# Two kept buffers for the preparation of w_out, earlier stores of its plain forms, and new block names in an attention and feed-forward kernel

## The chip, the cores and the metric

The kernel runs on one core of a Trainium2 chip. The metric is device time in microseconds of one execution, as the median of several runs. The core has a matmul engine (TensorE, PE; its weight loads are listed as PEld), a vector engine (VectorE, DVE), a scalar engine (ScalarE, ACT), a general engine (GpSimd, POOL) and a queue engine (SyncE, SP) that here only issues DMAs.

## What is computed

```
scores = (q @ k^T) / sqrt(64) - log(448)          # 8 batches, 12 heads, 448 positions, 64 wide
attn   = sigmoid(scores) @ v                      # 3584 tokens x 768
h      = attn @ w_in                              # 768 -> 2048
g      = max(0.01 * h, h)
out    = g @ w_out                                # 2048 -> 768
```

All inputs and the output are float32. The weights come to the kernel as 64-bit words and are turned into float32 on the chip.

## The kernel before, in words

**Number format.** Every operand of a large matmul is split into a high part (a cast on ScalarE) and a low part (the difference, on VectorE), and each product is three matmuls: high by high, high by low, low by high (`parts_mm`). A matmul has 448 columns.

**Fewer products.** Both weight matrices are multiplied by schemes that need fewer block products than the plain one, at the price of sums of blocks. For w_in (stage 2) a quad of four results takes seven products (`ORDER`, class `Quad`). For w_out (stage 3) 24 forms, blocks of w_out and sums of them, meet operands that are blocks of `g` and sums of them, in 26 products for each half of the tokens; the tables `PRODUCTS`, `MADE`, `STEPS` and `BLOCKS` say which. `MADE[p % 2]` lists the sums of `g` blocks (`s0` to `s7`) that stage 2 makes and stores for stage 3.

**Three stages in the order of program, cut in slots.**
1. Attention: 24 rounds of five slots, two head pairs each (tiles `qk`, `qks`, `sc`, `s`, `pv`, `x`).
2. First weight (class `First`): four groups `q` of 56 slots; a slot is nine matmuls, two slots a product, seven products a quad `u` of four. It loads prepared w_in forms (`wx`), splits them (`w`), and its results (`c11`, `c21`, `c22`, `c12`, shown as `c_h`) go through the leaky maximum on ScalarE and are stored to the DRAM tensors `g`. Sums of them (`MADE`, tiles `s`) are made on VectorE some slots later, by `later`, and stored too. Both kinds of tile share `st`, a pool of seven buffers. In the last quad of each group the sums are put off by `LATER` = 4 slots (`z`). The stores of the very last quad go on ScalarE's DMA queue, all others on SP's.
3. Second weight: 52 products of 36 matmuls, alternating between the PSUM accumulators `A` and `B`. The forms of w_out are loaded from the DRAM tensor `t1` (shown as `t`), the operands from `g`; `load`, `whole` (the sum, tile `gf`), `high` and `low` make an operand ready. The first operands are loaded and split in the last slots of stage 2 (list `todo`); the buffers they use are seven (`gp`), and eight more (`op`) that take the place of stage 2's tiles.

**The preparation of the weights** (`prep`) runs on VectorE beside stages 1 and 2, a few instructions a slot. For each of 8 parts `u` of w_in, then of w_out, it loads four raw pieces (`wr`), decodes each with five instructions into a quarter of the tile `wd`, forms sums and stores them: `firsts` for w_in, `second` for w_out. `second` walks through `STEPS`; `("sum", n, fn, to, x, y)` makes `n` blocks of 192 columns, side `d` is the decoded tile `wd` and side `s` the tile `ws`; `("store", side, i, n, form)` stores `n` blocks as forms from `form` on; `("wait",)` is a pause. In the kernel before, `wd` and `ws` are taken anew from a pool of two buffers for each `u`, all decoding comes first, then the first sums, then two stores of eight blocks, the pause, sums written over the blocks of `wd`, and a third store of eight blocks.

**What sets the order.** Each engine runs its instructions in the order of program (`keep_in_program_order`), and so does SP with its DMAs; semaphores make an instruction wait for data and for buffers. The generator `prep` yields after every instruction, and empty turns are yielded in a pause: `rest()` gives `WAIT` = 9 of them before slot 100 and `REST` = 4 after. `prepare` (attention) and `fill` (stage 2) ask the generator for its next turns: `fill` up to four times in a slot, as long as its running account of VectorE's work, `queue`, is under 1.6 us.

Of the kernel before, what the change touches and what calls it, by code (L numbers as in the profile page):

```python
# [10 lines left out]
F32 = mybir.dt.float32  # L11
# [17 lines left out]
READY, LEAD = 2, 2  # L29
# [1 line left out]
PACES = 4, 5, 4.2, 2.8, 2  # L31
TIMES = 1.92, 1.92, 2.33, 2.33, 1.66
PRODUCT, LESS, MOST = 1.8, 0.2, 4
WAIT, REST = 9, 4
ALONE = 100
LATER = 4
IDLE = 7
# [4 lines left out]

RAW = "00", "01", "30", "31", "10", "11", "20", "21"
MADE = (
    (("s0", "add", "30", "31"), ("s1", "add", "10", "20"), ("s2", "add", "00", "30"), ("s3", "add", "s0", "00"), ("s4", "add", "s3", "01")),
    (("s0", "add", "10", "20"), ("s1", "add", "20", "21"), ("s2", "add", "30", "31"), ("s3", "add", "00", "30"), ("s4", "add", "s0", "21"), ("s5", "add", "s2", "00"), ("s6", "add", "s5", "01"), ("s7", "add", "s4", "11")))


PRODUCTS = (
# [13 lines left out]
FORMS = 24  # L63
BLOCKS = "01", "20", "31", "10", "21", "00", "11", "30"
STEPS = (
# [12 lines left out]


def part(i):  # L80
# [14 lines left out]
def attn_ffn_kernel(ctx: ExitStack, tc: tile.TileContext, qk, v, w_in, w_out, out):  # L95
# [66 lines left out]
    def later(slots, *fns, first=False):  # L162

        chores.setdefault(now + slots, ([], []))[not first].extend(fns)
# [182 lines left out]
    def rest():  # L347

        return (None for _ in range(WAIT if now < ALONE else REST))

    def second(u, dec):


        n = len(BLOCKS)
        size = wide // 2
        e, at = u // 2, u % 2 * size
        both = {"d": dec.rearrange("p a b -> p (a b)").rearrange("p (n m) -> p n m", n=n),
                "s": block(F32, (n, size), f"ws1_{u}")}

        def of(n, side, at, step):  # L360
            x = both[side]
            if step == 0:
                return x[:, at:at + 1].broadcast_to((P, n, size))
            end = at + (n - 1) * step + (1 if step > 0 else -1)
            return x[:, at:end if end >= 0 else None:step]

        for what, *x in STEPS:
            if what == "wait":
                yield from rest()
            elif what == "store":  # L370
                side, i, n, form = x
                dma(out=t2d[:, form:form + n, e, at:at + size], in_=both[side][:, i:i + n])
            else:
                n, fn, *x = x
                to, x, y = (of(n, *z) for z in x)
                if fn == "neg":
                    vec_st(out=to, in0=x, scalar=-1.0, in1=y, op0=ALU.mult, op1=ALU.subtract)
                else:
                    (add if fn == "add" else sub)(to, x, y)
                yield  # L380

    def prep():
# [21 lines left out]
        yield  # L404
        for at, (m, k) in enumerate(pieces):
            w, u = todo[m]
            if k == 0:
                dec = block(F32, (4, HW), f"wd{w}_{u}")
            raw = raws[at]
            size = 4 * HW // n  # L410
            low, high = raw[:, :, 0], raw[:, :, 1]
# [13 lines left out]
                load()  # L425
            if now < ALONE:
                yield
            if k < n - 1:
                continue
            if w == 1:  # L430
                yield from second(u, dec)
            else:
                yield from firsts(u, dec)
            prepared.add((w, u))
            yield from rest()

    preps = prep()
    credit = 0.0
# [240 lines left out]
    class First:  # L679
# [26 lines left out]
        def after(self, quad, c, u, n):  # L706
# [21 lines left out]
            if n != 2:  # L728
                later(1, lambda: leaky(t, t))
            later(2 if n == 2 else 3, lambda: save(name(row, col), t))  # L730
            z = LATER if u == NU // 2 - 1 else 0
            have = set(c)
            i = 0
            for x in MADE[p % 2]:
# [135 lines left out]
    class Operand:  # L870
# [28 lines left out]
                else:  # L899
                    y.count[x] += 1  # L900

        def load(self):
            for x in self.new:
                h = self.raw[x] = Held(f"g{x}_{self.k}")
                dma(out=h.t.bitcast(F32), in_=gd[2 * self.p + int(x[0])][x[1:]])

# [70 lines left out]
    def g_load(k):  # L977

        nonlocal ahead
        room = SPARE + sum(x.needs() for x in operands[:k + 5] if x.x is None)  # L980
        while ahead < min(k + FAR + 1, total) and len(spare) >= len(operands[ahead].new) + room:
            operands[ahead].load()
            ahead += 1

# [1 line left out]
    todo = [(operands[k], "load") for k in range(READY)]  # L986
    for k in range(READY):
        todo += [(operands[k], what) for what in ("whole", "high", "low")]
    todo += [(operands[READY], "load")]
    ahead = READY + 1  # L990

    for k in range(NOP, size):
        m, at = divmod(k - NOP, 12)
        if m < WW[0] and at == 0:
            for n, what in ((0, "load"), (5, "high"), (7, "low")):
                later(n, getattr(weights[m], what))
        if k >= size - LEAD - len(todo) and todo:
            later(0, lambda x=todo.pop(0): getattr(*x)())
        slot(first.step)
    assert not todo  # L1000
    while chores:
# [142 lines left out]
```

## Time and profile before

| | |
|---|---|
| median of 3 runs | 1075.38 us (1072.38 to 1076.88) |
| profiled execution, its own time | 1073.51 us |
| its span | 1071.7 us |
| granted TensorE clock, mean | 0.986 |
| busy: PE, PEld, DVE, ACT | 1039.7, 870.3, 842.2, 583.7 us |
| HBM | 202.77 MB read, 96.86 MB written, 280 GB/s over the span |

In the profile's rows `out<-in` are the program's tile names without their numbers, and L132 is the line of the helper that records nearly every instruction, so rows are told apart by tiles. `t<-wd` and `t<-ws` are the stores of prepared weight forms, `g<-c_h` and `g<-s` those of stage 2's results and of their sums. In a timeline's row the bracket gives the idle time of the engine before the instruction and what ended it. A DMA group gives the size of each and the median time from issue to landing.

### The profile page before, as it was taken

Reading aid. Unit: us, or ns where it says so; the run is one execution under the profiler, and the core shown is the slowest. Engines: PE = TensorE matmul, PEld = TensorE weight load, DVE = VectorE, ACT = ScalarE, POOL = GpSimd, SP = SyncE. Lnnn points to the kernel's source line nnn. Section 1 sums busy time; section 2 is a strip of 40 time slices with the busy share of each in tenths; the row PEclk is TensorE's granted clock in tenths of the full one; section 3 lists DMA queues with packets and bytes.
Section 4 is the critical chain, followed back from the end, with each engine's and each line's share of the span. In section 5 each row is a group of like instructions: output and inputs, shape, how many; then the busy total and the mean of one; then the engine's idle time right before and its main releaser. Section 6 shows DMA issues by size and latency. Waiting matters only on the chain.

```text
span 1071.7 us, 15049 instructions
## 1 busy us (share of the span) xinstructions
PE 1039.7 (97%) x5738; PEld 870.3 (81%) x5738; DVE 842.2 (79%) x976; ACT 583.7 (54%) x610; POOL 0.3 (0%) x5
## 2 busy tenths in 40 slices
PE   9999999978999999998999999979999999999998
PEld 5555555534998999987989999969999999999997
DVE  5778888656979998977965566578998888899883
ACT  6877778756544754544545555555444625544440
POOL 0000000000000000000000000000000000000000
PEclk9999999988999999998999999989999999999999
DMA  8888788678789989989886788996669798666923
GB/s 302 286 286 280 258 269 291 233 263 266 264 269 320 324 290 305 341 307 345 278 288 209 255 298 295 363 392 273 255 227 310 276 368 332 267 255 229 312 110 128
DMA packets 113335, 300.62 MB, mean 280 GB/s; under 512 B 9200, under 2 KB 51312, under 8 KB 113264
## 3 DMA queue, kind: packets, MB, share of 16 engines
q1 hardware_dynamic: 111248, 295.19, 77.9%
q10 hardware_dynamic: 2016, 4.47, 1.1%
q8 instruction: 45, 0.74, 0.3%
q14 instruction: 26, 0.21, 0.1%
HBM read 202.77 MB, written 96.86 MB: 280 GB/s over the span
## 4 chain that ended last, share of the span: by engine, by line
PE 85%; DVE 6%; DMA 6%; issue 1%; ACT 1%; SPq 0%; ACTq 0%; DVEq 0%
PE px_h L132 19%; PE acc_B L132 17%; PE acc_A L132 16%; PE pv L132 10%; PE sc L132 9%; PE pz_h L132 8%; PE py_h L132 5%; DMA t<-wd 3%; DMA g<-s 2%; DVE wd L132 2%; DMA wx<-t 1%; DVE w L132 1%; DVE s L132 1%; DVE c_h L132 1%; DVE gf L132 1%
## 5 line engine op out<-in xcount | busy, mean ns | idle before, releaser
L132 PE MATMUL px_h<-hi,w 128*128 128x448 f32 x768 | 229.0, 369 | 12.3 <-DVE c_h L132 6.6
L132 PEld LDWEIGHTS px_h<-hi,w 128*128 128x128 f32 x768 | 146.9, 192 | 25.8 <-issue 8.5
L132 PE MATMUL acc_A<-gh,w 128*128 128x448 f32 x528 | 151.7, 362 | 0.0
L132 PE MATMUL px_h<-lo,w 128*128 128x448 f32 x384 | 141.0, 367 | 0.0
L132 DVE TENSOR_TENSOR w<-wx,w 128x768 fp32r<-128x768 f32 x112 | 106.8, 954 | 42.6 <-ACT w L132 42.5
L132 ACT ACTIVATE s<-sc 128x896 f32<-128x896 f32 x144 | 119.7, 932 | 18.3 <-PE sc L132 18.3
L132 PE MATMUL acc_B<-gh,w 128*128 128x448 f32 x416 | 121.8, 367 | 5.6 <-ACT o L132 4.9
L132 PE MATMUL pv<-s,v 128*64 128x448 f32 x576 | 113.8, 543 | 0.0
L132 PE MATMUL pz_h<-hi,w 128*128 128x448 f32 x384 | 113.2, 362 | 0.0
L132 PEld LDWEIGHTS sc<-qks 64*128 64x128 f32 x876 | 81.6, 190 | 32.0 <-issue 16.9
L132 PE MATMUL sc<-qks 64*128 64x448 f32 (+1 forms) x876 | 97.7, 373 | 7.9 <-DVE qks L132 7.6
L132 PEld LDWEIGHTS acc_A<-gh,w 128*128 128x128 f32 x528 | 98.9, 187 | 6.5 <-ACT o L132 0.4
L132 ACT ACTIVATE c_h<-c_h 128x896 f32<-128x896 f32 x48 | 45.8, 954 | 97.3 <-DVE c_h L132 97.3
L132 ACT CAST w<-wx 128x768 fp32r<-128x768 f32 x112 | 91.7, 833 | 8.0 <-DMA wx<-t 8.0
L132 DVE TENSOR_TENSOR w<-w 128x1536 fp32r<-128x1536 f32 x52 | 91.0, 1752 | 0.0
L132 PEld LDWEIGHTS pv<-s,v 128*64 128x64 f32 x576 | 39.1, 137 | 63.3 <-issue 54.3
L132 PEld LDWEIGHTS acc_B<-gh,w 128*128 128x128 f32 x416 | 79.3, 191 | 11.5 <-ACT o L132 5.3
L132 PE MATMUL acc_B<-g,w 128*128 128x448 f32 x328 | 85.8, 365 | 0.0
L132 PEld LDWEIGHTS px_h<-lo,w 128*128 128x128 f32 x384 | 73.6, 192 | 4.7
L132 ACT CAST w<-w 128x1536 fp32r<-128x1536 f32 x52 | 76.6, 1475 | 0.1
L132 PEld LDWEIGHTS pz_h<-hi,w 128*128 128x128 f32 x384 | 71.9, 188 | 5.1
L132 DVE SCALAR_TENSOR_TENSOR wd<-wr,wd 128x384 int32<-128x384 int32 x128 | 71.3, 557 | 3.3
(98 smaller groups left out, 1583.3 us busy)
## 6 DMA issues: line engine op xcount, KB each, us to landing
wx<-t SPq DMA_DIRECT2D x112, 384.0 KB, 5.1
w<-t SPq DMA_DIRECT2D x52, 768.0 KB, 4.3
g<-g SPq DMA_DIRECT2D x34, 896.0 KB, 7.3
g<-c_h SPq DMA_DIRECT2D x60, 448.0 KB, 4.7
g<-s SPq DMA_DIRECT2D x48, 448.0 KB, 5.3
qk<-in_qk SPq DMA_DIRECT2D x46, 448.0 KB, 5.2
g1s<-g SPq DMA_DIRECT2D x18, 896.0 KB, 6.6
wr<-in_w_in SPq DMA_DIRECT2D x32, 384.0 KB, 4.9
```

What stands on the lines that cost most here:

```text
L132: return lambda *args, **kw: tc.keep_in_program_order(issue(*args, **kw))
```

## The change

`second` gets two buffers that are taken once, for `u` = 0, and swapped for each following `u`: what was side `s` is decoded into next. It is called after each decoded piece `k`: `PLAIN` says that nothing follows piece 0, that blocks 0 to 3 are stored as they are after piece 1, and blocks 4 and 5 after piece 2; `STEPS` follows piece 3. `STEPS` has 14 sums where it had 12, over the same 18 blocks, and five stores; with those of `PLAIN` a part `u` has seven stores of 192 to 576 KB where it had three of 768 KB, and the same 24 blocks. `REST` is 1, and no rest follows a part of w_out. The blocks of w_out have another order (`BLOCKS`), the blocks of results other names in `PRODUCTS`, and the sums of odd groups in `MADE` are made from other blocks; the number and shapes of products and sums in stages 2 and 3 are the same. The last quad of the last group no longer puts its sums off. `todo` loads two more operands (the second only in its first block), so all of `todo` begins two slots earlier.

```
-WAIT, REST = 9, 4
+WAIT, REST = 9, 1
...
 MADE = (
-    (("s0", "add", "30", "31"), ("s1", "add", "10", "20"), ...),
-    (("s0", "add", "10", "20"), ("s1", "add", "20", "21"), ("s2", "add", "30", "31"), ("s3", "add", "00", "30"), ("s4", "add", "s0", "21"), ("s5", "add", "s2", "00"), ("s6", "add", "s5", "01"), ("s7", "add", "s4", "11")))
+    (("s0", "add", "30", "31"), ("s1", "add", "20", "10"), ...),
+    (("s0", "add", "21", "11"), ("s1", "add", "11", "10"), ("s2", "add", "31", "30"), ("s3", "add", "01", "31"), ("s4", "add", "s0", "10"), ("s5", "add", "s2", "01"), ("s6", "add", "s5", "00"), ("s7", "add", "s4", "20")))
...
-    (4, "A", True, ("+1s4",), ("c010", "c100", "c110")), (16, "B", True, ("+001",), ("c101",)),
+    (9, "A", True, ("+1s4",), ("c011", "c100", "c111")), (17, "B", True, ("+001",), ("c101",)),
...
-BLOCKS = "01", "20", "31", "10", "21", "00", "11", "30"
+BLOCKS = "00", "01", "21", "30", "10", "11", "20", "31"
+PLAIN = {0: (), 1: (("store", "d", 0, 4, 0),), 2: (("store", "d", 4, 2, 4),)}
 STEPS = (
-    ("sum", 3, "sub", ("s", 0, 1), ("d", 0, 1), ("d", 2, 1)),
-    ("sum", 1, "neg", ("s", 3, 1), ("d", 3, 1), ("d", 6, 1)),
-    ("sum", 2, "sub", ("s", 4, 1), ("d", 6, 0), ("s", 1, -1)),
-    ("sum", 1, "sub", ("s", 6, 1), ("s", 4, 1), ("d", 4, 1)),
-    ("sum", 1, "sub", ("s", 7, 1), ("s", 0, 1), ("s", 1, 1)),
-    ("sum", 1, "sub", ("d", 3, 1), ("d", 3, 1), ("d", 5, 1)),
-    ("sum", 1, "neg", ("d", 2, 1), ("d", 7, 1), ("d", 2, 1)), ("store", "s", 0, 8, 0), ("store", "d", 0, 8, 8),
-    ("wait",), ("sum", 1, "add", ("d", 4, 1), ("d", 2, 1), ("d", 4, 1)),
-    ("sum", 2, "neg", ("d", 7, -6), ("d", 3, -2), ("d", 7, -3)),
-    ("sum", 2, "add", ("d", 2, 1), ("d", 2, 1), ("d", 0, 6)),
-    ("sum", 1, "neg", ("d", 5, 1), ("d", 2, 1), ("d", 5, 1)),
-    ("sum", 2, "sub", ("d", 6, -6), ("d", 4, -4), ("d", 7, -4)), ("store", "d", 0, 8, 16))
+    ("sum", 3, "sub", ("s", 5, 1), ("d", 1, 3), ("d", 7, -1)), ("store", "s", 5, 3, 11),
+    ("sum", 2, "sub", ("s", 3, 1), ("d", 2, 0), ("s", 6, -1)),
+    ("sum", 1, "sub", ("s", 1, 1), ("s", 5, 1), ("s", 6, 1)),
+    ("sum", 1, "sub", ("s", 2, 1), ("s", 3, 1), ("d", 5, 1)),
+    ("sum", 1, "neg", ("s", 0, 1), ("d", 6, 1), ("d", 2, 1)), ("store", "s", 0, 5, 6),
+    ("sum", 1, "sub", ("d", 6, 1), ("d", 6, 1), ("d", 0, 1)),
+    ("sum", 1, "neg", ("d", 7, 1), ("d", 3, 1), ("d", 7, 1)), ("store", "d", 6, 2, 14), ("wait",),
+    ("sum", 1, "add", ("d", 5, 1), ("d", 7, 1), ("d", 5, 1)),
+    ("sum", 2, "neg", ("d", 3, 1), ("d", 6, -2), ("d", 3, 2)),
+    ("sum", 1, "add", ("d", 2, 1), ("d", 6, 1), ("d", 2, 1)),
+    ("sum", 1, "add", ("s", 7, 1), ("d", 7, 1), ("d", 1, 1)),
+    ("sum", 1, "sub", ("d", 1, 1), ("d", 1, 1), ("d", 2, 1)),
+    ("sum", 1, "neg", ("d", 0, 1), ("s", 7, 1), ("d", 0, 1)),
+    ("sum", 1, "sub", ("s", 6, 1), ("d", 5, 1), ("d", 3, 1)), ("store", "d", 0, 6, 16), ("store", "s", 6, 2, 22))
...
-    def second(u, dec):
+    def second(u, k, dec):
...
-        both = {"d": dec.rearrange("p a b -> p (a b)").rearrange("p (n m) -> p n m", n=n),
-                "s": block(F32, (n, size), f"ws1_{u}")}
+        both = {side: dec[i].rearrange("p a b -> p (a b)").rearrange("p (n m) -> p n m", n=n) for i, side in enumerate("ds")}
...
-        for what, *x in STEPS:
+        for what, *x in PLAIN.get(k, STEPS):
...
-            if k == 0:
+            if k == 0 and w == 0:
                 dec = block(F32, (4, HW), f"wd{w}_{u}")
+            elif k == 0:
+                both = [block(F32, (4, HW), f"wd{w}_{i}") for i in range(2)] if u == 0 else both[::-1]
+                dec = both[0]
...
-            if k < n - 1:
-                continue
             if w == 1:
-                yield from second(u, dec)
-            else:
+                yield from second(u, k, both)
+            elif k == n - 1:
                 yield from firsts(u, dec)
-            prepared.add((w, u))
-            yield from rest()
+            if k == n - 1:
+                prepared.add((w, u))
+                if w == 0:
+                    yield from rest()
...
-            z = LATER if u == NU // 2 - 1 else 0
+            z = LATER if u == NU // 2 - 1 and p < NQ - 1 else 0
...
-        def load(self):
-            for x in self.new:
+        def load(self, n=None):
+            for x in self.new[len(self.raw):n]:
...
-        while ahead < min(k + FAR + 1, total) and len(spare) >= len(operands[ahead].new) + room:
+        while ahead < min(k + FAR + 1, total) and len(spare) >= len(operands[ahead].new) - len(operands[ahead].raw) + room:
...
-    todo += [(operands[READY], "load")]
-    ahead = READY + 1
+    todo += [(operands[READY + n], "load", *part) for n, part in ((0, ()), (1, ()), (2, (1,)))]
+    ahead = READY + 2
...
-            later(0, lambda x=todo.pop(0): getattr(*x)())
+            later(0, lambda x=todo.pop(0): getattr(*x[:2])(*x[2:]))
```

More of the change, by code (lines that the diff above doesn't have):

```diff
@@ L44 @@
 MADE = (
-    (("s0", "add", "30", "31"), ("s1", "add", "10", "20"), ("s2", "add", "00", "30"), ("s3", "add", "s0", "00"), ("s4", "add", "s3", "01")),
-    (("s0", "add", "10", "20"), ("s1", "add", "20", "21"), ("s2", "add", "30", "31"), ("s3", "add", "00", "30"), ("s4", "add", "s0", "21"), ("s5", "add", "s2", "00"), ("s6", "add", "s5", "01"), ("s7", "add", "s4", "11")))
+    (("s0", "add", "30", "31"), ("s1", "add", "20", "10"), ("s2", "add", "00", "30"), ("s3", "add", "s0", "00"), ("s4", "add", "s3", "01")),
+    (("s0", "add", "21", "11"), ("s1", "add", "11", "10"), ("s2", "add", "31", "30"), ("s3", "add", "01", "31"), ("s4", "add", "s0", "10"), ("s5", "add", "s2", "01"), ("s6", "add", "s5", "00"), ("s7", "add", "s4", "20")))
 PRODUCTS = (
[13 rows of a table removed]
[13 rows of a table added]
 FORMS = 24
-BLOCKS = "01", "20", "31", "10", "21", "00", "11", "30"
+BLOCKS = "00", "01", "21", "30", "10", "11", "20", "31"
+PLAIN = {0: (), 1: (("store", "d", 0, 4, 0),), 2: (("store", "d", 4, 2, 4),)}
 STEPS = (
[12 rows of a table removed]
[14 rows of a table added]
 def part(i):
```

24 rows, old and new, of the table PRODUCTS are left out of this document.

## The prediction

> **What bounds the kernel now.** I read the page's first part, then the chain of waits, then TensorE's timeline for its gaps, then VectorE's timeline for what stood before each gap.
>
> ```profile
> PE 1039.7 (97%) x5738; PEld 870.3 (81%) x5738; DVE 842.2 (79%) x976; ACT 583.7 (54%) x610; POOL 0.3 (0%) x5
> ```
>
> TensorE is busy 97% of the span, so only gaps, and what slow clock follows them, can be won. Its timeline shows the gaps over 1 us after the start-up (the answers to its stretches of 10 us; in brackets the idle time before and what ended it). The first row is stage 2's first product.
>
> ```profile
> 259.93 0.48 PE L132 MATMUL px_h<-hi,w 128*128 128x448 f32 x1
> ```
>
> ```profile
> 211.69 1.88 PE L132 MATMUL sc<-qks 64*128 64x448 f32 x16 [1.27 <-DVE qks L132]
> 239.17 1.11 PE L132 MATMUL sc<-qks 64*128 64x448 f32 x4 [6.35 <-DVE qks L132]
> 265.23 1.11 PE L132 MATMUL px_h<-hi,w 128*128 128x448 f32 x2 [4.62 <-DVE w L132]
> 496.57 0.71 PE L132 MATMUL px_h<-hi,w 128*128 128x448 f32 x1 [4.50 <-DVE c_h L132]
> 551.61 0.44 PE L132 MATMUL px_h<-hi,w 128*128 128x448 f32 x1 [2.14 <-DVE c_h L132]
> 709.87 0.74 PE L132 MATMUL acc_B<-gh,w 128*128 128x448 f32 x1 [4.94 <-ACT o L132]
> ```
>
> Five of the six were ended by VectorE. VectorE's own timeline says why it was late:
>
> ```profile
> 208.29 0.36 DVE L132 TENSOR_TENSOR wd<-wd 128x192 f32<-128x192 f32 x1 [6.05 <-DMA t<-wd]
> 237.23 0.36 DVE L132 TENSOR_TENSOR wd<-wd 128x192 f32<-128x192 f32 x1 [10.49 <-DMA t<-wd]
> 263.95 0.36 DVE L132 TENSOR_TENSOR wd<-wd 128x192 f32<-128x192 f32 x1 [7.26 <-DMA t<-wd]
> 475.33 0.36 DVE L132 TENSOR_TENSOR wd<-wd 128x192 f32<-128x192 f32 x1 [5.94 <-DMA t<-wd]
> 492.00 1.09 DVE L132 TENSOR_TENSOR s<-s,c_h 128x896 f32<-128x896 f32 x1 [4.91 <-DMA g<-s]
> 549.51 0.36 DVE L132 TENSOR_TENSOR wd<-wd 128x192 f32<-128x192 f32 x1 [4.58 <-DMA t<-wd]
> ```
>
> The waits by engine give the total:
>
> ```profile
> DVE wd L132 <- DMA t<-wd: 43.0, 8, 10.5
> ```
>
> Eight waits, one for each eighth `u` of w_out: the first in-place sum of `STEPS` after its "wait" overwrites the decoded blocks while their store is still reading them. All VectorE work behind it (the attention's `qks`, the weights' low halves, `c_h`) stands in line.
>
> **What each place costs.** The chain of waits (start, length, what) gives the points between which time is lost:
>
> ```profile
> 179.52 3.84 PE sc L132 x36
> ...
> 189.69 3.84 PE sc L132 x36
> ...
> 227.10 10.04 DMA t<-wd
> ...
> 270.58 3.60 PE py_h L132 x18
> ...
> 506.26 3.60 PE py_h L132 x18
> ...
> 560.64 3.60 PE py_h L132 x18
> ...
> 679.44 3.61 PE px_h L132 x18
> ...
> 720.92 7.20 PE acc_A L132 x36
> ```
>
> TensorE's own pitch stands in the same rows: 10.17 us for a round of attention (179.52 to 189.69), 0.2 us a matmul (3.60 for 18), so 25.2 for a unit of seven stage-2 products and 7.2 for a stage-3 product of 36. Against it:
>
> - T1, end of the attention: six rounds from 189.69 would end at 250.7; stage 2 begins at 259.93: 9.2 lost.
> - T2, first product of stage 2: 259.93 to 270.58 is 10.65 for 18 matmuls of 3.6: 7.05 lost.
> - T4, 270.58 to 506.26: 235.68 for nine units (226.8): 8.88, nearly all at the 496 gap.
> - T5, 506.26 to 560.64: 54.38 for two units (50.4): 3.98.
> - 560.64 to 679.44 is 33 times 3.6: nothing lost.
> - T7, stage 2 to 3: from 683.04 (679.44 and one product) to 720.92 is 37.88 for four products (28.8): 9.08.
>
> Together 38.2 us; with all of it gone the profiled execution's 1073.5 would be 1035.3.
>
> The losses exceed the gaps since the clock falls after them (PEclk is the seventh column group's figure, ahead of the DMA share):
>
> ```profile
> 200.00:265.00 65.00, 52.74 (x374) 28.10 (x372) 38.55 (x83) 41.04 (x53) 0.00 (x0) 0.93 0.78 258
> 340.00:440.00 100.00, 100.00 (x502) 93.73 (x501) 91.54 (x126) 57.87 (x67) 0.00 (x0) 1.00 0.91 311
> 235.20:242.00 6.80, 2.83 (x16) 2.52 (x18) 4.70 (x9) 1.41 (x2) 0.00 (x0) 0.50 0.28 100
> 552.60:556.00 3.40, 3.40 (x11) 3.00 (x10) 2.81 (x5) 1.52 (x2) 0.00 (x0) 0.50 0.48 149
> ```
>
> After the 6.35 gap 6.8 us ran at 0.50, after the 2.14 gap 3.4 us: T5's 3.98 is the 2.14 and about 1.7 of half clock, and I count both as gone. The Trainium skill's page "TensorE: Matmul & The Clock Gate" (section "HAM oscillation — how this bites in real kernels") asks for "no PE-idle gaps >~3.4µs"; by that rule the 2.14 gap would not have cost any clock, T5 would be worth 2.1 and the sum 1.8 higher. This trace disagrees: the 0.50 stands in the row.
>
> **The change, part by part.** *Kept buffers, plain forms stored early.* The plain blocks d0 to d3 are stored after decode piece 1, d4 and d5 after piece 2, s5 to s7 after the first sum. The first sum behind the pause writes d5, whose store now has five decode operations and seven sums between, where before it had nothing but the pause. So the eight waits go or shrink. VectorE's balance in 200 to 265 agrees that they are T1 and T2: it worked 38.55 us and waited 6.05 + 10.49 + 7.26 = 23.8, together 62.4 of 65, while the undisturbed pitch leaves some 51; without the waits it has slack.
>
> What comes in their place: s7 is rewritten ten turns after its store, and the next `u`'s decode writes s0, s1 ten turns after theirs. The prices are these (ns, least, median and most; first and last start):
>
> ```profile
> L132 DVE TENSOR_SCALAR wd<-wd x128: 351/360/364, 18.5 to 525.7; 128x384 f32<-128x384 f32 x64, 128x384 int32<-128x384 int32 x64
> L132 DVE SCALAR_TENSOR_TENSOR wd<-wr,wd x128: 548/558/580, 19.3 to 527.4; 128x384 int32<-128x384 int32 x128
> ...
> L132 SPq DMA_DIRECT2D t<-wd x24: 360/377/1002, 30.6 to 553.6; - x24
> L132 DVE TENSOR_TENSOR ws<-wd,ws x24: 550/553/559, 31.1 to 528.8; 128x384 f32<-128x384 f32 x24
> ...
> L132 DVE TENSOR_TENSOR ws<-ws x8: 350/351/353, 201.3 to 530.7; 128x192 f32<-128x192 f32 x8
> ```
>
> ```profile
> t<-ws SPq DMA_DIRECT2D x8, 768.0 KB, 4.9
> ...
> v<-in_v SPq DMA_DIRECT2D x4, 192.0 KB, 4.2
> ```
>
> Ten turns are nine sums and the pause: one or two of 0.553 and the rest of 0.351, 3.4 to 3.6 us of VectorE's own time, some 5 (an estimate) with the attention's work between, against a landing of 4.2 to 4.9 (10.04 at the worst, at 227.10 in the chain). So 0 to 5 us of wait may stay in each of the attention's last three `u`; the gaps above were 2 to 5 us shorter than the waits before them, so most of this is covered. I take 2.0 left of T1 and T2's 16.25, with 0 and 8 as ends. In stage 2 the turns come slower (a slot of 1.8 us, shared), ten turns are over 10 us: of the in-place waits T4 and T5 keep 0.5 each.
>
> *Two more sums for each `u`.* Both halves still sum 10 and 8 blocks, but the second half takes seven instructions for five: 6 x 0.351 + 0.553 for 2 x 0.351 + 3 x 0.553, 0.3 us more, 2.4 in all, on VectorE alone.
>
> *REST 4 to 1, no rest behind a `u`.* A pause of four empty turns uses up one slot's filling; two of these go for each `u`, of about 26 slots ((530.7 - 201.3) / 7 / 1.8). A `u` takes four pieces of 3 x 0.36 + 2 x 0.558 and sums of some 5.5, 14.3 us in its 47, a third of VectorE's work there. It gets some 8% denser: 91.5 busy in 340 to 440 becomes about 95. That cover is thin; if it breaks TensorE waits for low halves. I take 1.0, ends 0 and 6.
>
> *Seven stores for three.* 32 more DMAs of the same total size on SP, 0.377 us of issue each, 12 us of its 350 there. Loads of weights queue behind a store that waits for VectorE, as before. I take nothing, ends -1 (the bursts of 1.5 MB that took 10 us become smaller) and 8.
>
> *MADE renamed for odd q.* At T4 the wait is for a store of a just made form: `s4` needed a buffer of the seven `st`, and only that of a form stored 6 us before was free. The new sums need "21", "11", "10", which come two products earlier, so the old quad's buffers are free before the next quad takes its own; and VectorE is no longer late by 5.94. Both speak for T4 going; I leave 1.5 beside the 0.5, ends 0 and 8.
>
> *z = 0 for the last quad, operand loads ahead.* At T7:
>
> ```profile
> 700.09 2.03 DVE L132 TENSOR_TENSOR gf<-g,g 128x1792 f32<-128x1792 f32 x1 [5.75 <-DMA g<-s]
> ```
>
> ```profile
> 704.21 1.69 ACT L132 CAST g1s<-gf 128x1792 fp32r<-128x1792 f32 x1 [6.81 <-DVE gf L132]
> 705.80 2.84 ACT L132 CAST w<-w 128x1536 fp32r<-128x1536 f32 x2
> 708.55 1.27 ACT L132 COPY o<-acc_B 128x1344 f32<-128x1344 f32 x1
> ```
>
> The fourth product waits for the PSUM copy at 708.55, which stands on ScalarE behind the cast of `gf`, which waits for the landing of the last made form. With the new sums three of the four forms need nothing of the last product, so the last is added some 2.5 us earlier, and its store runs ahead of the loads that share the DMAs. The two loads themselves were issued about then already (TensorE's last stage-2 products were still running), so I give their move nothing. I take 4 us off T7's 9.08, ends 9 and -5. Shapes and numbers of products, copies and output stores do not change with the new names: zero.
>
> Sum: 38.2 - (T1 and T2 2.0, T4 2.0, T5 0.5, T7 5.1, density 1.0) = 27.6 saved; 1073.5 - 27.6 = 1045.9. The median of the runs, 1075.38, stands 1.9 above the profiled execution's 1073.51; between 1045.9 and 1047.8 I say 1047.
>
> **The rivals.** *New waits for old* (0.18): the ten turns are too short in the attention's end, half of T1 and T2 stays (8), the dense preparation costs 3, T7 stays as it is: about 15 saved instead of 28, 1059. For it: VectorE's work and landing times are nearly equal there; against it: the 10 us landing came when 1.5 MB were stored at once.
>
> *Small stores crowd the DMAs* (0.10): the share is already 0.91 in 340 to 440, and 192 KB land hardly faster than 768 KB, so 32 more landings are 140 us of landing time. If weights' loads then come 1 to 2 us late in every other `u`, it takes 8 back and T4 and half of T7 stay: 1073.5 - 28 + 8 + 7 + 2 = 1062.5. The Trainium skill's page "DMA: Bandwidth & Descriptors" (section "Measured (HBM→SBUF, 128 partitions, SWDGE, issued from GpSimd)") speaks for this side: "Batch DMAs to ≥1 MiB for ≥75% of peak". The rows of 192 and 768 KB agree with it in kind; that path is another than this kernel's.
>
> *Slower* (0.04): the kept buffers are one tile for all eight `u`, and if an operation that writes one block had to wait for every store out of that tile, each of seven stores would hold VectorE for a landing: 8 x 7 x 4.5 = 252 us for the 43 now. It decides as soon as more than three waits of 4.5 stay for each `u` (the slack of 8 us in 100 is then used up); the full price is over 1200. Against it stands the end of the kernel, where both halves of one tile are written without a pause though the first half's store is queued between:
>
> ```profile
> 1061.76 0.69 DVE L132 TENSOR_TENSOR o<-o,acc_one 128x224 f32<-128x224 f32 x2 [0.85 <-PE acc_one L132]
> ```
>
> *No change* (0.03): the waits merely move to the next `u`'s first decode, at the same length.
>
> **How the numbers follow.** The forecast has 0.65, from 1036 to 1053 by its own ends. The range reaches up through the first rival and most of the second: 1037 to 1063. A measurement here tells 0.5% (5 us) from no change. Faster: 0.65 + 0.18 + 0.07 of the second rival; the same: 0.03 of it and 0.03; slower: 0.04.
>
> **What would show it.** Right: the row of `wd` waiting for `t` under 10 us; stage 2's first product before 253 and its next within 5 us; no gap over 1 us in the rest of stage 2; fewer stretches at 0.50. The preparation's last decode ends relative to the products some 12 slots (20 us) earlier. Wrong: VectorE waits for `t` inside decode rows; ScalarE's `w` waiting for `wx` more than now; VectorE over 97% in mid stage 2 with TensorE waiting for `w`; a stage change of more than 9 us.

## The result and the profile after

The changed kernel took **1047.20 us** in the median of 4 runs (1044.46 to 1049.28); the kernel before, beside it on the same chip, 1075.18 us (1072.38 to 1076.88). The ratio is **0.9741 [0.9709, 0.9772]**: 2.6% faster, where 1047 (1037 to 1063) was forecast. The profiled execution of after is the slowest of its four, 1049.28 us by its own time (span 1047.2); against the 1073.51 of the one profiled before it is 24.2 us shorter, by the spans (1071.7 and 1047.2) 24.5, and that difference is what is split up below.

The page's first part, after:

```profile
PE 1032.3 (99%) x5738; PEld 865.6 (83%) x5738; DVE 844.9 (81%) x992; ACT 583.9 (56%) x610; POOL 0.3 (0%) x5
```

Two rows of the waits by engine (us in all, times, longest). The eight waits of 43.0 us for stores of `wd` are two of 7.1:

```profile
DVE wd L135 <- DMA t<-wd: 7.1, 2, 3.7
DVE gf L135 <- DMA g<-s: 2.1, 1, 2.1
```

TensorE's gaps, in its timeline: all those over 1 us after the start-up, and ahead of them the first product of stage 2.

```profile
254.00 0.48 PE L135 MATMUL px_h<-hi,w 128*128 128x448 f32 x1
```

```profile
236.22 2.11 PE L135 MATMUL sc<-qks 64*128 64x448 f32 x18 [2.24 <-DVE x L135]
256.70 0.68 PE L135 MATMUL px_h<-hi,w 128*128 128x448 f32 x2 [2.02 <-DVE w L135]
268.94 0.67 PE L135 MATMUL pz_h<-hi,w 128*128 128x448 f32 x2 [1.15 <-DVE w L135]
684.87 0.47 PE L135 MATMUL acc_B<-gh,w 128*128 128x448 f32 x1 [2.05 <-ACT o L135]
686.61 1.11 PE L135 MATMUL acc_B<-gh,w 128*128 128x448 f32 x2 [1.07 <-DVE w L135]
```

Ahead of the first two of them VectorE's timeline has the two waits, both at the fourth sum behind the pause, the one that writes `s7` (joined in one row with the next sum):

```profile
233.41 0.75 DVE L135 TENSOR_TENSOR wd<-wd 128x192 f32<-128x192 f32 x2 [3.65 <-DMA t<-wd]
254.76 0.75 DVE L135 TENSOR_TENSOR wd<-wd 128x192 f32<-128x192 f32 x2 [3.48 <-DMA t<-wd]
```

The chain of waits gives the points for the sum:

```profile
28.63 3.84 PE sc L135 x36
...
211.63 3.84 PE sc L135 x36
...
226.68 6.71 DMA t<-wd
248.00 6.74 DMA t<-wd
...
272.41 3.60 PE px_h L135 x18
...
661.21 7.20 PE acc_A L135 x36
...
696.45 7.20 PE acc_A L135 x36
```

From 211.63 four rounds of 10.17 would end at 252.3, and four products more at 266.7; the fifth product starts at 272.41, so T1 and T2 together kept 5.7. From there to stage 3's first product at 661.21 are 388.8 us, 108 products of 3.6 without any loss: T4, T5 and the term for density are zero. Stage 3's first four products take 35.24 instead of 28.8, so 6.44 is left of T7. Together 12.1 of 38.2. This execution also began its third round 1.6 us later than the one before (28.63 against 27.02 in the chain of before). 38.2 - 12.1 - 1.6 is 24.5, the difference of the two spans (1071.7 and 1047.2).

### The profile page after: what moved, and what is told of

The parts are those of the page before. It is cut to its first block, busy times and chain, and to the rows that moved or that the text cites. A ratio compares the mean times of both kernels' runs of the same rounds, so it can differ in the third digit from the quotient of the medians.

```text
span 1047.2 us, 15127 instructions
## 1 busy us (share of the span) xinstructions
PE 1032.3 (99%) x5738; PEld 865.6 (83%) x5738; DVE 844.9 (81%) x992; ACT 583.9 (56%) x610; POOL 0.3 (0%) x5
## 4 chain that ended last, share of the span: by engine, by line
PE 94%; DVE 3%; DMA 1%; issue 0%; ACT 0%; ACTq 0%; DVEq 0%
PE px_h L135 21%; PE acc_A L135 18%; PE acc_B L135 18%; PE pz_h L135 11%; PE pv L135 11%; PE sc L135 10%; PE py_h L135 5%; DVE wd L135 2%; DMA t<-wd 1%; PE acc_one L135 0%; DVE w L135 0%; DVE lo L135 0%; DVE qks L135 0%; DVE x L135 0%; DVE gf L135 0%
## 5 line engine op out<-in xcount | busy, mean ns | idle before, releaser
L135 PE MATMUL px_h<-hi,w 128*128 128x448 f32 x768 | 223.6, 362 | 2.0 <-DVE w L135 2.0
L135 PEld LDWEIGHTS px_h<-hi,w 128*128 128x128 f32 x768 | 143.8, 187 | 11.9 <-DVE w L135 2.4
```

What stands on the lines that cost most here:

```text
L135: return lambda *args, **kw: tc.keep_in_program_order(issue(*args, **kw))
```

## The experiments

Each edit was timed against the kernel before in three rounds. The table has for each the median, the ratio with its interval, VectorE's wait for stores of `wd` in all (by the rows that name such a store), and where TensorE lost time in the profiled execution, by the first matmuls of the stages in its trace: the end of the attention (from the round that starts near 128 us to stage 2's first matmul, less 12 rounds of 10.166), stage 2 (less 403.2) and stage 3 (to its last matmul, less 374.4; this count gives T7 some 0.2 us less than the rows above). A value below zero shows how exact the count is.

| kernel | us | ratio | `wd` waits | attention | stage 2 | stage 3 |
|---|---|---|---|---|---|---|
| before | 1075.18 | | 43.0 | 9.3 | 19.8 | 8.9 |
| after | 1047.20 | 0.9741 [0.9709, 0.9772] | 7.1 | 1.8 | 3.8 | 6.2 |
| e1_fresh | 1058.98 | 0.9846 [0.9822, 0.9870] | 14.0 | 8.4 | 9.1 | 6.8 |
| e2_plain_late | 1051.67 | 0.9785 [0.9770, 0.9800] | 8.1 | 5.2 | 3.2 | 8.4 |
| e3_rest4 | 1045.18 | 0.9721 [0.9703, 0.9739] | 2.1 | 0.2 | 0.1 | 9.0 |
| e4_before_pause8 | 1060.98 | 0.9870 [0.9855, 0.9885] | 28.3 | 7.6 | 11.2 | 6.8 |
| e5_before_later2 | 1058.54 | 0.9858 [0.9842, 0.9874] | 43.3 | 9.9 | 12.9 | 0.9 |
| e7_todo_old | 1042.91 | 0.9713 [0.9695, 0.9731] | 7.2 | 1.7 | 4.0 | 3.7 |
| e8_boundary | 1044.23 | 0.9724 [0.9709, 0.9738] | 6.2 | 1.2 | 3.5 | 3.7 |
| e9_both | 1042.26 | 0.9702 [0.9684, 0.9720] | 1.4 | -0.6 | 0.1 | 8.1 |
| e10_best | **1036.65** | 0.9636 [0.9620, 0.9652] | 2.1 | -0.3 | 0.3 | 1.1 |
| e11_before_z0 | 1074.76 | 0.9995 [0.9986, 1.0005] | 42.9 | 11.0 | 18.7 | 8.7 |
| e12_z_old | 1045.97 | 0.9733 [0.9712, 0.9754] | 5.0 | 3.6 | 1.3 | 5.5 |
| e13_place | 1037.70 | 0.9639 [0.9610, 0.9668] | 2.9 | 0.0 | 0.5 | 3.5 |

The theory for the first two columns of losses: what counts is the distance between a store and the next writing of the block that it reads. The rival: the number of bytes stored at once, or how VectorE's work is spread.

**e1_fresh**, the changed kernel, but its two buffers taken anew for each `u`, without the swap:

```
-both = [block(F32, (4, HW), f"wd{w}_{i}") for i in range(2)] if u == 0 else both[::-1]
+both = [block(F32, (4, HW), f"wd{w}_{u}_{i}") for i in range(2)][::(1, -1)[u % 2]]
```

> The changed kernel, but with two buffers taken anew for each part u of w_out (in the same places and roles) in place of the two kept ones. Theory A (the time came from keeping every write of VectorE far behind the store that reads the same blocks): a buffer taken anew is free only when all stores out of its old tile have landed, the last of them (s6, s7) issued just ahead, so VectorE waits for t at the start of each u, 7 times some 4 to 6 us, 25 to 45 us in all as in the kernel before (43.0), and TensorE loses most of T1, T2, T4, T5 again: 1060 to 1072. Rival B (the time came from the pacing, REST 1 and no rest, and from the new sums): the stores are as early and the pauses as short as in the changed kernel, so 1045 to 1050.

It lost 11.8 us against after, a little less than expected, and the waits are of the kind expected, with 25.3 us in all at the low end of the size. Two stand at the sums behind the pause, as in after, 5.4 us. The others stand at the first decode of each of the seven later `u`, where after has none: four name a store, 8.6 us in all, and three name nothing (`issue`), 11.3 us. Each of these three ends 0.08 us behind the landing of a store of six blocks (at 216.60, 319.96 and 410.98 by the landing times in the trace). The table counts the rows that name a store, 14.0:

```profile
216.68 0.36 DVE L135 TENSOR_SCALAR wd<-wr 128x384 int32<-128x384 int32 x1 [4.95 <-issue]
241.47 0.36 DVE L135 TENSOR_SCALAR wd<-wr 128x384 int32<-128x384 int32 x1 [3.17 <-DMA t<-wd]
264.18 0.36 DVE L135 TENSOR_SCALAR wd<-wr 128x384 int32<-128x384 int32 x1 [2.56 <-DMA t<-wd]
```

So decoding into a kept buffer, which waits block by block, is worth more than a tile taken anew, whose first decode waits. The waits grew by 18.2 us and the time by 11.8: eight gaps of TensorE of 0.9 to 2.2 us stand in the attention's last rounds and at stage 2's first products, and only one of 0.7 behind them in stage 2.

**e2_plain_late**, the changed kernel with the six plain blocks stored together ahead of the first sum:

```
-PLAIN = {0: (), 1: (("store", "d", 0, 4, 0),), 2: (("store", "d", 4, 2, 4),)}
+PLAIN = {0: (), 1: (), 2: ()}
 STEPS = (
+    ("store", "d", 0, 6, 0),
```

> The changed kernel, but the six plain blocks d0 to d5 are stored together behind the last decoded piece, in front of the first sum (six stores for each u, not seven). Theory A: d5 is overwritten eight turns after its store and not twelve or more, so in the attention's last three parts VectorE waits 2 to 4 us at d5 for a store of 576 KB, in place of the 3.6 at s7; in stage 2 eight turns are still over 8 us and nothing is lost: 1046 to 1053. Rival B (storing the plain forms at decode is what took the waits away): most of the eight waits come back, 30 us of wait and more, 1060 to 1070.

As expected in time, 4.5 us over after, and in place; the wait at 230.20 is longer than the 2 to 4 us expected, 5.07 (3.65 in after). Ahead of stage 3 the early storing of the plain forms is worth 2.8 us (8.4 lost for 5.6); stage 3 gave the rest of the loss (8.4 for 6.2), for the reason that e13_place shows below.

**e3_rest4**, the changed kernel with `WAIT, REST = 9, 4`: the pause has three empty turns more, in the attention's last 20 slots and in stage 2.

> The changed kernel with REST 4, so the pause is about a slot longer. Theory A: the two waits of 3.6 us for t in the attention's end become 1.5 to 2 us, T1 and T2 keep 2 to 4 us instead of 5.7; stage 2 has nothing to win: 1043 to 1047. Rival B (the denser preparation is part of the gain): slower by a few us, 1050 to 1055, with the gaps of TensorE back in stage 2.

One wait of 2.1 us is left, and from the attention's end to stage 3 nothing is lost:

```profile
231.59 0.36 DVE L135 TENSOR_TENSOR wd<-wd 128x192 f32<-128x192 f32 x1 [2.13 <-DMA t<-wd]
```

Three empty turns closed the distance that was 3.5 us too short. The median fell by only 2.0, as stage 3 lost 2.7 more: the 5.3 won before it were half given back at its start.

**e4_before_pause8**, the kernel before with a pause of 8 turns ahead of the sums that overwrite, and 1 turn behind each `u`:

```
-                yield from rest()
+                yield from rest(8)
...
             prepared.add((w, u))
-            yield from rest()
+            yield from rest(1)
```

> The kernel before with 8 empty turns in the pause of STEPS and 1 behind a part u (it was 4 and 4), from slot 100 on; nothing else. Theory A: the in-place sum stands a slot further behind the stores of 1.5 MB, so of 43.0 us of wait some 20 stay; where the wait falls under 4 us TensorE loses nothing: T1 and T2 keep about 8 of 16, T5 goes, T7 stays, 1058 to 1066. If T4 comes from VectorE being late (theory lag) it goes too; if it comes from the seven buffers of st (theory buffers) the wait of s for g<-s, 4.9 us, stays. Rival B: the pause is no cause, and the time stays within 5 us of 1075.

The two pauses so changed are worth 14 us without any new buffer, 10.3 of it ahead of stage 3 by the table. The waits fell less than expected, to 28.3 us and not to some 20. T4's gap did not go with the shorter waits; it grew. In VectorE's timeline and in TensorE's:

```profile
486.38 2.22 DVE L132 TENSOR_TENSOR s<-s,c_h 128x896 f32<-128x896 f32 x2 [9.18 <-DMA g<-s]
```

```profile
490.61 0.71 PE L132 MATMUL px_h<-hi,w 128*128 128x448 f32 x1 [5.86 <-DVE c_h L132]
```

**e5_before_later2**, the kernel before with `LATER = 2`, so that the sums of `g` blocks are put off by fewer slots and their seven buffers come free sooner:

> The kernel before with LATER 2, so the sums of each group's last quad are made two slots earlier, before the next quad takes its own tiles of st; nothing else. Theory buffers (T4 is a shortage of the seven st tiles): the wait of s for g<-s, 4.9 us at 492, and TensorE's gap of 4.5 us with its half clock go, while the eight waits for t (43 us in all, +-4) stay: T4 falls from 8.9 to 1 or 2, 1066 to 1070. Theory lag (VectorE is late there since it waited 5.9 us for t at 475): the gap stays as long as that wait stays, 1073 to 1077.

The waits for stores of `wd` stayed, and T4's wait and gap went:

```profile
DVE wd L132 <- DMA t<-wd: 43.3, 8, 10.5
```

T4 is the shortage of the seven buffers `st`, as the prediction had it, not the late VectorE. The time fell below what was expected since stage 3's loss fell too, from 8.9 to 0.9, which nothing in the theory said. That opened the question of stage 3.

**e7_todo_old**, the changed kernel with the old list of loads in the last slots of stage 2 (one operand ahead, not two and a block):

```
-todo += [(operands[READY + n], "load", *part) for n, part in ((0, ()), (1, ()), (2, (1,)))]
-ahead = READY + 2
+todo += [(operands[READY], "load")]
+ahead = READY + 1
```

> The changed kernel with the list of operand loads at the end of stage 2 as it was (no two loads more). Theory of the prediction: these loads were issued at about the same time anyway, so the time stays within 2 us of 1047 and T7 at 6 to 9 us. Rival: put ahead of the last stores they are what shortened T7 (9.1 to 6.4), and without them T7 is 9 or more and the time 1049 to 1052.

A miss: the two loads ahead cost time. The DMA groups of the stretch in which the last results are stored show it, first after (661 to 667.5), then e7 (659 to 664): size of each and median time to landing.

```profile
g<-s ACTq DMA_DIRECT2D x4, 448.0 KB, 9.4
...
g<-c_h ACTq DMA_DIRECT2D x2, 448.0 KB, 5.7
```

```profile
g<-s ACTq DMA_DIRECT2D x4, 448.0 KB, 8.1
...
g<-c_h ACTq DMA_DIRECT2D x2, 448.0 KB, 2.6
```

With the loads ahead, the last stores land later, and stage 3 loses 2.5 us more.

**e8_boundary**, the changed kernel with another order of work beside stage 3's second and third product, so that ScalarE's cast of the fifth product's sum `gf` no longer stands ahead of the cast of the fourth product's weights:

```
+            if k == 1:
+                operands[4].whole()
+            elif k == 2:
+                weights[3].high()
+                operands[4].high()
+                weights[4].high()
...
```

> The changed kernel with another order of work in the second and third product of stage 3: the PSUM copy that frees B, and the split of the form for the fourth product, stand ahead of the cast of the fifth product's operand sum. Theory A for T7 (the fourth product is late since its PSUM copy stands on ScalarE behind the cast of gf, which waits for a late store): the gap of 2 us and more at the fourth product goes, with it the 3.4 us of half clock, T7 falls from 6.4 (up to 9) to under 2: 1040 to 1043. Rival (the loads of 401 GB/s themselves are late, so the product waits for its form or its operand instead): T7 stays within 2 us, 1045 to 1049.

Half a success, with 1044.23 between the two ranges: the gap at the fourth product went and one came a product later.

```profile
691.32 0.44 PE L135 MATMUL acc_A<-g1s,w 128*128 128x448 f32 x1 [3.32 <-DVE o L135]
```

**e9_both**, that order together with `REST` 4:

> The changed kernel with REST 4 and with the new order of work at the start of stage 3. Theory A: what each saves adds up, since they lie in different stages: REST 4 keeps T1 and T2 under 1 us, the new order keeps T7 under 2 us: 1037 to 1040, with 1035 as what is left when nothing is lost. Rival for T7: no better than REST 4 alone, 1044 to 1047.

A miss, between the two ranges. What `REST` won before stage 3 was lost in it again (8.1): `gf` now waited 9.28 us. The order of the casts is not what is late; `gf` is. Its row in VectorE's timeline names a load of weights, but in the chain a store of `s` stands ahead of it, which landed 0.1 us before `gf` began:

```profile
656.96 15.86 DMA g<-s
672.93 2.04 DVE gf L135
```

**e10_best**, the changed kernel with both parts as before that had cost time, `REST` 4 and the old list of loads:

> The changed kernel with two of its parts as they were: REST 4, and the old list of loads in the last slots of stage 2. If the two costs are separate (the waits for stores at the end of the attention and at stage 2's first products, 5.4 us; the last stores held up by two more operand loads, some 4 us), stage 2 loses under 0.5 us against its pitch, stage 3 about 3.7 as with the old list alone, and the time is 1037 to 1040. Rival: what is won before stage 3 is taken back at its start, where the preparation of the operands then comes closer to the last products: stage 3 loses 7 or more and the time stays at 1041 to 1043.

The fastest of all, 10.6 us below after and a little below the range. In VectorE's timeline `gf` does not wait for a store any more:

```profile
664.74 2.02 DVE L135 TENSOR_TENSOR gf<-g,g 128x1792 f32<-128x1792 f32 x1
667.49 2.03 DVE L135 TENSOR_TENSOR gf<-gf,g1s 128x1792 f32<-128x1792 f32 x1 [0.73 <-DMA g1s<-g]
```

**e11_before_z0** and **e12_z_old** change one line, which says whether the very last quad puts its sums off: the kernel before without it, the changed kernel with it.

```
-            z = LATER if u == NU // 2 - 1 else 0
+            z = LATER if u == NU // 2 - 1 and p < NQ - 1 else 0
```

> The kernel before, with the sums of the very last quad no longer put off (z = 0 there alone). If it is the putting off that makes stage 3 late, its loss of 8.9 us falls to 2 or less as with LATER 2, everything else stays (waits of VectorE for stores 43 us, the gap of 4.5 at 496), and the time is 1066 to 1069. Rival: the loss fell with LATER 2 because the quads before were also put off by less, or since other landings are as late: 6 us or more of it stay and the time is 1072 to 1076.

> The changed kernel, but the very last quad's sums put off by four slots as in the kernel before. If not putting them off is what took some of the loss off the start of stage 3, that loss (6.2 us) rises by 2.5 to 5 us and the time is 1049 to 1053. Rival: the two loads ahead set the landing of the last stores in any case, and the loss and the time stay as they are, 1046 to 1048.

In both cases the rival: no change. The reason lies in the programs, not in the DMAs. What was put off beyond the last slot is done right at its end, and the two programs of each pair have the same instructions in the same order on every engine. So e12_z_old is a second execution of after, and the two show how far single places repeat: 1.8 and 3.8 us lost in the one, 3.6 and 1.3 in the other. Their medians, 1047.20 and 1045.97, lie 1.2 us apart, so a difference of that size between two kernels here tells nothing.

**e13_place.** `gf` (the sum for the fifth product; the fourth stands behind its cast through the copy on ScalarE) adds three blocks of the first two groups, stored long before. It reads nothing of the last stores, and yet it starts when one of them lands. What the two share is a place: the pool `op`, in which `gf` is made, lies where stage 2's tiles lay, the buffers of `st` among them. The experiment has `REST` 4 as in e3_rest4, where `gf` waited longest, and lays the eight tiles of `op` out with the one of `gf` first:

```
+    for n in (6, 0, 1, 2, 3, 4, 5, 7):
+        op.tile([P, KQ, S], F32R, tag=f"o{n}", name=f"place_{n}")
     spare.extend((op, f"o{n}") for n in range(8))
```

> The changed kernel with REST 4, and the eight tiles of the pool op laid out in another order: the one in which the sum gf of stage 3's fourth product is made comes first, and no longer lies where the last sums s of stage 2 lay. With REST 4 alone the sum waited 7.2 us, started 17.5 us after stage 3's first product, right behind the landing of the very last store, and stage 3 lost 9.0 us. It reads nothing of that store. If the wait was for the place, it starts 12.5 us after the first product or earlier, stage 3 loses 3 us or less, and the time falls from 1045.2 to 1036 to 1040. Rival: the last stores and loads fill the DMAs and the sum's own operands are as late: stage 3 loses 6 or more and the time is 1043 to 1047.

VectorE's timeline, first of e3_rest4 and then of e13_place:

```profile
671.12 2.03 DVE L135 TENSOR_TENSOR gf<-g,g 128x1792 f32<-128x1792 f32 x1 [7.17 <-DMA g<-s]
```

```profile
666.36 2.02 DVE L135 TENSOR_TENSOR gf<-g,g 128x1792 f32<-128x1792 f32 x1
```

The wait is gone, 12.1 us after stage 3's first matmul (654.26) instead of 17.5, while the last store landed as late as ever (17.1 us after it, 17.4 in e3_rest4, by the landing times in the traces). Stage 3 lost 3.5, a little more than the bound of 3, and the time fell by 7.5 to 1037.70 (by 4.8 between the two profiled executions), as the theory of the place said. The chain of e13_place shows what is late next: a load of weights and the copy behind it.

```profile
662.42 12.70 DMA w<-t
676.62 1.18 ACT o L135
677.85 9.07 PE acc_B L135 x36
```

The same reading fits the other kernels: `gf` starts 17.2 us after the first matmul in the kernel before, 17.5 in e3, 14.0 in after, 12.7 in e7, 10.6 in e10, and stage 3 loses 8.9, 9.0, 6.2, 3.7, 1.1. In the first two it goes behind the landing of the fourth and last store of `s`, in after and e7 behind the third, in e10 behind none. The addresses in the built programs say the same: `gf` has one place in all of them but e13_place, over two of the seven buffers. The tiles last made there are `s4` and `s7` in the kernel before, `s1` and `s7` in e3 and e9, `c21` and `s4` in after, e7 and e8, `c12` and `s1` in e10, and `s0` and `s1` in e5, whose stage 3 lost only 0.9. `s0`, `s1`, `s4` and `s7` are stored in this order, and in all these kernels but e10 and e5, where the stores had landed before, `gf` starts 0.1 to 0.2 us behind the landing of the later of its two. So `REST`, `LATER` and the list of loads all change which tiles lie there. Why each of them gives just the tiles that it gives was not followed further; the order in which the buffers are asked for is the same in after and e3.

## Why the prediction was right, and where it was not

**T1 and T2**: the mechanism held, the sizes did not. The forecast had 2.0 us left, measured are 5.7, within its ends of 0 and 8. The prediction named the place: `s7` is rewritten ten turns after its store. It took some 5 us of turns against a landing of 4.2 to 4.9, and both sides were off. The two stores land after 6.7 us (226.68 and 248.00 in the chain); the sum ahead of `s7` is done 3.1 and 3.3 us behind their issue, so waits of 3.65 and 3.48 us remain, one in each of two `u`. The first row is the first sum of the first of the two `u`, the others are the sums just ahead of the two waits:

```profile
224.60 0.76 DVE L135 TENSOR_TENSOR wd<-wd 128x576 f32<-128x576 f32 x1
229.41 0.35 DVE L135 TENSOR_TENSOR wd<-wd 128x192 f32<-128x192 f32 x1
250.93 0.35 DVE L135 TENSOR_TENSOR wd<-wd 128x192 f32<-128x192 f32 x1
```

The first sum of the other `u` ends at 247.97, so its turns took 3.3 us. In the first `u` they took 4.4, but its store was issued 1.3 us after its sum was done: SP had two loads to issue first. The landing was taken from the medians of two DMA groups; the eight stores of this size (288 KB) in after have a median of 4.7 too, but land after 2.3 to 8.6 us. This stretch keeps the DMAs 88% busy:

```profile
190.00:260.00 70.00, 65.75 (x482) 36.02 (x475) 54.69 (x120) 49.58 (x63) 0.00 (x0) 1.00 0.88 294
```

So are they in 340 to 440 us, where two of these stores landed after 4.7 and 4.8 us, so this share alone does not tell how long a landing takes. The 10.04 us row, which the prediction called the worst, warned that it can stretch.

**T4 and T5**: 0 and 0, where 2.0 and 0.5 were left. That T4 is a buffer of `st` is shown by e4 (it stays when the waits for `wd` shrink) and e5 (it goes when they don't); that the new sums let the old quad's buffers go sooner agrees with the rows of after, but no run has the new `MADE` alone.

**`REST` and density**: 1.0 was set down, measured is 0. In 340 to 440 us VectorE worked 92.7 us, where about 95 was expected and 91.5 was before. But the forecast looked for the cost of `REST` = 1 in stage 2's slots, and it lay in the pause itself: the ten turns count it, and e3_rest4, with thirteen, lost only 0.3 us where after lost 5.6.

**T7**: 5.1 was left by the forecast, 6.4 measured, and the working behind it was wrong in three steps. "Waits for the landing of the last made form" (the prediction's words on the cast of `gf`) read the row's releaser as the data; e13_place shows that it is the place. The 4 us put down to `z` and to earlier sums cannot come from `z`, which changes no instruction (e11, e12); by the starts of `gf` above, stage 3's loss fell since `gf` in after lies on other tiles, whose last store lands earlier. And "the two loads themselves ... I give their move nothing": without them the kernel is 4.3 us faster (1042.91 against 1047.20), and with `REST` 4 it is 8.5 (e10 against e3), there by way of the place of `gf`.

**Seven stores for three, two more sums**: at zero, as put down; no row of after shows a wait of ScalarE's `w` or of SP that costs TensorE a gap in stage 2.

**The rivals.** "New waits for old" has the time of e1_fresh almost to the microsecond (1058.98, where 1059 was said), that is of the change without its kept buffers, but by luck: there the attention and stage 2 lost 17.5 us, where the rival had 8 and 3, and stage 3 lost 6.8, where it had 9. The small stores did not crowd the DMAs (their share in 340 to 440 us is 0.88, and 0.91 was before), the tile is waited for block by block, and the waits did not move into the decoding.

**The total.** It came out nearer than its terms: 3.5 us of caution at T4, T5 and density stood against 3.7 too little at T1 and T2 and 1.3 at T7. That is luck, and so is that the median meets 1047 to 0.2 us: the profiled execution, for which 1045.9 was worked out, took 1049.28, 1.6 of the difference by its later start.

**The signs.** Of those named for being right, the waits for `t` came under 10 us (7.1), the clock fell in one stretch (behind 684.87) and not in five, the end of the kernel aside, and the last decode starts some 28 us earlier against stage 3's first product than before. Not met: stage 2's first product at 254.00 and not before 253, its next 6.0 us later and not within 5, and the gap of 1.15 us at 268.94. All three stand where T1 and T2 stand, and 1.6 us of the first is the later start. None of the signs of being wrong came.

## What to carry to other kernels

A tile that is rewritten needs a distance in time from the issue of its store to the rewriting that covers a long landing of such a store, not the median of the run (here 4.7 us in the median and up to 8.6); a few empty turns at the right place gave as much here as a buffer. Where an instruction waits for a transfer whose data it does not read, look at what its tile lies on: the order in which a pool's tiles are laid out was worth 7.5 us, without a transfer more or less. Loads put ahead of a stage change are not free when the stage's last stores must land first.

## What the chip showed that was not expected

**The clock after short gaps.** Three gaps of nearly one length in after were followed by different clocks. Stretches behind the gaps at 236.22 (2.24), 256.70 (2.02) and 684.87 (2.05); the granted clock is the figure after the engines, ahead of the DMA share:

```profile
236.40:243.00 6.60, 6.60 (x46) 3.15 (x50) 6.25 (x15) 4.09 (x5) 0.00 (x0) 1.00 0.98 293
256.80:263.00 6.20, 6.20 (x31) 5.82 (x32) 6.10 (x12) 2.78 (x3) 0.00 (x0) 1.00 1.02 335
685.40:692.40 7.00, 5.93 (x17) 5.14 (x17) 7.00 (x5) 2.58 (x2) 0.00 (x0) 0.53 1.01 416
```

Only the third cost clock. The 2.14 us gap of before, too, had half clock behind it, so a gap's length alone does not tell. The third one is the only of the three with a second gap (1.07) within 2 us, but the one of before has none, so that does not decide either. The Trainium skill's page "TensorE: Matmul & The Clock Gate" (section "HAM oscillation — how this bites in real kernels") gives a length of about 3.4 us as the bound for a gap; two of these three agree with it and one does not.

The traces do tell more. The granted clock of all fourteen changes only at whole multiples of 3.41 us from its first change in the same trace (in before at 6.47, 235.16, 241.99, 262.47, 269.30, 494.58 and so on). Cut into such steps, the first gap falls partly into one step and partly into the next, 1.22 and 1.01 us; the second likewise, 1.00 and 1.01. The third lies in one step with the start of the gap behind it, 2.28 us idle, and the gap of before in one step, 2.14. The first gap's two steps and the one behind them, then the third gap's step and the two behind it:

```profile
231.80:235.21 3.41, 2.19 (x22) 1.61 (x18) 1.76 (x4) 3.16 (x5) 0.00 (x0) 1.00 1.00 360
235.21:238.62 3.41, 2.40 (x20) 1.81 (x22) 3.27 (x9) 1.60 (x3) 0.00 (x0) 1.00 0.82 263
238.62:242.00 3.38, 3.38 (x20) 1.29 (x18) 3.17 (x9) 2.69 (x4) 0.00 (x0) 1.00 0.98 306
682.36:685.77 3.41, 1.14 (x5) 0.39 (x3) 3.41 (x3) 3.31 (x3) 0.00 (x0) 1.00 1.02 425
685.77:692.60 6.83, 5.99 (x16) 5.34 (x17) 6.83 (x5) 2.21 (x2) 0.00 (x0) 0.50 1.01 415
```

Of the steps at full clock in the fourteen traces, from the first change on and up to the end of TensorE's work, none with 1.71 us idle or less was followed by half clock, and of the 28 with 1.79 us or more all but one (1.84, in e8_boundary). So what a gap of some 2 us costs depends on where it falls.

**Landings at a stage change.** In the 35 us of stage 3's start the DMAs are busy all the time and move 402 GB/s; a store of 448 KB, which landed in 2.6 us in e7's first microseconds of that stage (the DMAs 70% busy in 659.4 to 662), takes 9.4 there, and the load of weights in e13_place's chain took 12.7:

```profile
661.00:696.40 35.40, 32.28 (x147) 29.22 (x146) 26.28 (x16) 19.29 (x14) 0.00 (x0) 0.90 1.01 402
```
